# Packed softmax for six of eight units of a windowed attention that feeds an MLP

## The chip, the core and the metric

The kernel runs on one core of a Trainium2 chip. The metric is the device time of a run in microseconds; before the change three runs gave 794.72, 796.49 and 797.60 us. The profiler's own execution took 798.29 us, of which 796.3 lie between the first and the last instruction (the span). The engines are named as the profile names them: PE is TensorE (matmuls; PEld are its weight loads), DVE is VectorE, ACT is ScalarE, POOL is GpSimd, SP is SyncE, which only issues transfers here.

## The reference

Attention of 4 batches x 8 heads over 768 positions with head size 64; each query sees the first `n_sink` = 4 keys and the last `window` = 128 keys up to its own. What comes out goes, as 3072 tokens of width 512, through an MLP with a leaky ReLU.

```python
scores = scale * np.matmul(q, k.transpose(0, 1, 3, 2))
keep = is_sink | in_window                     # pos < n_sink, 0 <= rel < window
scores = np.where(keep, scores, -1000000000.0)
a = np.exp(scores - np.max(scores, axis=-1, keepdims=True))
a = a / (np.sum(a, axis=-1, keepdims=True) + 1e-09)
x = np.matmul(a, v)                            # then (B*S, H*D)
h = x @ w_in                                   # 512 -> 2048
out = np.maximum(0.01 * h, h) @ w_out          # 2048 -> 512
```

## The kernel before

**Units.** The work is cut into 8 units (`NU`): a batch has two, its first 384 queries (half 0) and its last 384 (half 1). A unit has 4 pairs of heads (`NPAIR`) and three query tiles of 128 (`T`). A query tile sees two key blocks of 128, the one before its own and its own, and the 4 sink keys: a score tile is 128 x 260 (`W3`), columns 0 to 127 the block before, 128 to 131 the sinks, then its own block. The first tile of half 0 sees only its own block (128 columns).

**Attention of a pair.** `scores` (L220 for the first two units, which are "native": fp32 products, two heads side by side; L225 for the others, where a head's q and k were split by `split_head` into a high part and a remainder) writes a tile into bank `s0` or `s1`. L235 on VectorE adds the mask, keeps the negative row maximum `negm` and writes `pk`; L239 on ScalarE takes the exponential and the row sum `sm`. L242 on GpSimd copies the 4 sink columns out to `sk`. `turn` transposes each 128 x 128 block of `pk` on TensorE (L260) into bank `t`, and L266 or L268 copies it to `pt` in SBUF. `gather` transposes `sk` (L274) into the same bank `t`, and L278 and L279 write it out as `st` in two parts; `gather` also inverts the sums (L283, L284) and spreads them (L286) to `rb`, which `spread` transposes (L293), again in bank `t`, and copies to `r`. `values` multiplies `pt` by the values (L306), adds the sink part (L310, one matmul), multiplies by `r` (L313) and splits the result into `xh` and `xl` (L316, L317), the inputs of the MLP.

**MLP of a unit.** For each of 16 blocks of 128 hidden columns: 12 matmuls of 384 columns into bank `h` (L399); L406 on ScalarE and L407 on VectorE form `g`; L408 on ScalarE and L409 form its two parts `gh` and `gl` (L409 is VectorE's for the first unit, GpSimd's later); one block later 9 matmuls of 512 columns (L421) add into the three output banks. The weights arrive as raw 64-bit words; during the opening and the first unit's MLP VectorE decodes each block in three steps (L125, L127, L129, all in the tile `w`), and ScalarE and GpSimd split it. In units 2 to 5 `check_weights` loads the raw words again, 32 blocks in all, and reduces them on ScalarE, GpSimd (L144) and VectorE (L146).

**What sets the order.** TensorE's order is written by hand: the program runs one step of `mlp_stream` after the other and between them, by the count `due`, steps of `attention_stream`, a few ahead of the unit that needs them. In `attention_stream` a step is a score tile, or one deferred function (`turn`, `gather`, `spread`, `values`) from the list `pend`, taken by a credit and a lag. The other engines' orders, SP's among them, come from the tile framework's scheduler; every engine works through its list in order. PSUM has 8 banks, each used by name: `h`, `s0`, `s1`, `t`, `v`, `o0`, `o1`, `o2`. SBUF tiles rotate by tag: `raw` (3 buffers, raw words and q/k), `io` (3, decoded words, output tiles, the check), `qksp`, `pk`, `pt`, `v`.

## Time and profile before

| | |
|---|---|
| median of 3 runs | 796.49 us (794.72 to 797.60) |
| profiled execution | 798.29 us, span 796.3 us |
| PE busy | 730.3 us, 92% |
| DVE, ACT, POOL busy | 403.9, 354.1, 377.5 us |
| mean clock granted to PE | 0.976 of full speed |
| DMA | 72.75 MB, mean 91 GB/s |

Busy time is the time in which at least one instruction of an engine runs. Matmuls overlap each other, so what one costs among others is the distance from its start to the next start. "Idle ... <- X" in a row means that the engine stood still and that X's end released it.

### The profile page before, as it was taken

The page shows a single profiled execution, that of the slowest core. Times are in us where ns is not written, and L with a number is a line of the kernel's source. Part 1 is how long each engine was busy: PE and PEld are TensorE (multiplying, and loading weights), DVE is VectorE, ACT ScalarE, POOL GpSimd, SP SyncE. Part 2 cuts the span into 40 slices and gives each one's busy share as a digit, 9 for nine tenths or more (in the row PEclk, how much of TensorE's full clock was granted, in tenths as well). Part 3 has the DMA queues.
Part 4 walks back from the last instruction along what each step waited for, and adds up shares of the span by engine and source line. Part 5 has one row for each costly group of instructions (what it writes and reads, how often), then busy time and mean ns, then how long its engine had stood idle before and what let it go on. Part 6 is the DMA issues. An engine that isn't in the chain of part 4 may idle for free. (4 is left out here: it accounts for less than half of the span.)

```text
span 796.3 us, 11589 instructions
## 1 busy us (share of the span) xinstructions
PE 730.3 (92%) x4109; PEld 614.6 (77%) x4109; DVE 403.9 (51%) x1070; ACT 354.1 (44%) x910; POOL 377.5 (47%) x473
## 2 busy tenths in 40 slices
PE   4798878999999899989999899998999999999996
PEld 3466666788888777878787788777788888888894
DVE  5979989753445444463444544445444544422111
ACT  3665545543444454454454454454454445322221
POOL 2525556434444655655655656545655544222221
PEclk9799999999999999999999999999999999999998
DMA  5626455221113423333322322224323220001001
GB/s 171 218 92 204 157 168 171 90 90 48 57 41 104 135 81 91 93 97 109 101 90 90 138 91 88 82 78 149 115 63 111 62 75 14 1 1 40 1 1 44
DMA packets 26034, 72.75 MB, mean 91 GB/s; under 512 B 3024, under 2 KB 5328, under 8 KB 25968
## 3 DMA queue, kind: packets, MB, share of 16 engines
q1 hardware_dynamic: 25824, 71.80, 27.8%
q8 instruction: 34, 0.56, 0.3%
q14 instruction: 32, 0.26, 0.1%
q10 hardware_dynamic: 144, 0.13, 0.0%
HBM read 65.63 MB, written 6.29 MB: 90 GB/s over the span
## 5 line engine op out<-in xcount | busy, mean ns | idle before, releaser
L399 PE MATMUL h<-xh,wih 128*128 128x384 f32 x512 | 185.0, 361 | 5.6 <-DVE g L407 5.4
L399 PE MATMUL h<-xl,wih 128*128 128x384 f32 x512 | 173.3, 338 | 0.0
L399 PE MATMUL h<-xh,wil 128*128 128x384 f32 x512 | 173.3, 338 | 0.0
L421 PE MATMUL o<-woh,gh 128*128 128x512 f32 x384 | 161.7, 421 | 0.0
L421 PE MATMUL o<-woh,gl 128*128 128x512 f32 x384 | 153.0, 398 | 1.8 <-DVE gl L409 1.5
L409 POOL TENSOR_TENSOR gl<-g,gh 128x384 fp32r<-128x384 f32 x112 | 113.4, 1013 | 84.8 <-ACT gh L408 83.8
L421 PE MATMUL o<-wol,gh 128*128 128x512 f32 x384 | 152.4, 397 | 0.0
L242 POOL COPY sk<-pk 128x36 f32<-128x36 f32 x160 | 45.4, 286 | 196.4 <-ACT pk L239 196.3
L407 DVE TENSOR_TENSOR g<-h,g 128x384 f32<-128x384 f32 x128 | 70.6, 552 | 122.9 <-ACT g L406 121.5
L235 DVE CUSTOM_DVE_ANT_0 pk<-s,m 128x260 f32<-128x260 f32 (+1 forms) x192 | 75.9, 402 | 112.2 <-PE s L225 102.8
L406 ACT ACTIVATE g<-h 128x384 f32<-128x384 f32 x128 | 62.3, 487 | 154.1 <-PE h L399 151.9
L239 ACT ACTIVATE pk<-pk,negm 128x260 f32<-128x260 f32 (+1 forms) x192 | 94.2, 491 | 58.9 <-DVE negm L235 58.7
L399 PEld LDWEIGHTS h<-xh,wih 128*128 128x128 f32 x512 | 97.7, 191 | 12.4 <-DVE g L407 7.5
L268 DVE COPY pt<-t 128x128 f32<-128x128 f32 (+1 forms) x168 | 67.0, 399 | 70.7 <-PE t L260 68.2
L399 PEld LDWEIGHTS h<-xl,wih 128*128 128x128 f32 x512 | 98.1, 192 | 3.3
L399 PEld LDWEIGHTS h<-xh,wil 128*128 128x128 f32 x512 | 97.3, 190 | 0.0
L421 PEld LDWEIGHTS o<-woh,gl 128*128 128x128 f32 x384 | 72.8, 190 | 20.2 <-DVE gl L409 2.4
L188 POOL TENSOR_TENSOR qksp<-qkraw,qksp 64x392 fp32r<-64x392 f32 (+1 forms) x48 | 57.3, 1194 | 64.1 <-issue 62.0
L408 ACT CAST gh<-g 128x384 fp32r<-128x384 f32 x128 | 65.4, 511 | 43.8 <-DVE g L407 40.7
L260 PE MATMUL t<-ident,pk 128*128 128x128 f32 x352 | 69.2, 284 | 11.6 <-DVE pt L268 11.5
L421 PEld LDWEIGHTS o<-woh,gh 128*128 128x128 f32 x384 | 72.9, 190 | 8.6 <-issue 0.7
L421 PEld LDWEIGHTS o<-wol,gh 128*128 128x128 f32 x384 | 73.2, 191 | 7.0
(88 smaller groups left out, 933.6 us busy)
## 6 DMA issues: line engine op xcount, KB each, us to landing
craw<-in_wq SPq DMA_DIRECT2D x32, 512.0 KB, 3.6
qkraw<-in_qk SPq DMA_DIRECT2D x24, 454.0 KB, 3.3
qkraw<-in_qk SPq DMA_DIRECT2D x24, 388.0 KB, 3.3
wiraw<-in_wq SPq DMA_DIRECT2D x16, 512.0 KB, 3.9
woraw<-in_wq SPq DMA_DIRECT2D x16, 512.0 KB, 3.6
out<-ob SPq DMA_DIRECT2D x23, 256.0 KB, 2.1
v<-in_vu SPq DMA_DIRECT2D x16, 256.0 KB, 2.7
v<-in_vu SPq DMA_DIRECT2D x16, 192.0 KB, 2.3
```

Source lines behind the costliest of these rows:

```text
L188: nc.gpsimd.tensor_tensor(out=sp[D:P, TU:TU + n], in0=raw[D:P, TU:TU + n], in1=sp[D:P, TU:TU + n].bitcast(F32), op=ALU.subtract)
L235: anchor[0] = nc.vector.tensor_tensor_reduce(out=w[:, 0:kn], in0=ps[:, 0:kn], in1=masks[min(T * (u % 2) + j, 2)], scale=-SCALE, scalar=3.0 ...
L239: nc.scalar.activation(out=w[:, 0:kn], in_=w[:, 0:kn], func=AF.Exp, scale=-1.0, bias=neg, accum_out=state["sm"][:, j, o:o + 1])
L242: nc.gpsimd.tensor_copy(out=state["sk"][:, j, :, o, :], in_=w[:, P:WM].rearrange("p (o s) -> p o s", o=1).broadcast_to([P, SKG, NSK]))
L260: nc.tensor.transpose(out=tp[:, i * m + c * P:i * m + (c + 1) * P], in_=w[:, a:z], identity=ident)
L268: nc.vector.tensor_copy(out=dst, in_=src)
L399: nc.tensor.matmul(ph[:, 0:TU], lhsT=w[:, cs], rhs=x, start=cc == 0 and c == 0, stop=cc == NCC - 1 and c == 2)
L406: nc.scalar.mul(g, ph[:, 0:TU], 0.01)
L407: anchor[0] = nc.vector.tensor_tensor(out=g, in0=ph[:, 0:TU], in1=g, op=ALU.max)
L408: nc.scalar.copy(out=gh, in_=g)
L409: (nc.gpsimd if u else nc.vector).tensor_tensor(out=gl, in0=g, in1=gh.bitcast(F32), op=ALU.subtract)
L421: nc.tensor.matmul(po[t], lhsT=gg[:, tsl], rhs=w, start=f == 0 and c == 0, stop=f == NFC - 1 and c == 2)
```

## The change

From the third unit on (`not native(u)`) the softmax of a tile is packed. A query at place q of its tile sees keys 0..q of its own block and keys q+1..127 of the block before, 128 in all, so both fit in one block: `copy_predicated` (L411) writes the scores of the block before over the own block's columns where key > query (mask `tri`), in PSUM, and `soft` works on 132 columns, the 4 sinks and the packed block. After a head's third tile the three row sums are inverted (L418, L419) and the three tiles multiplied by them in one instruction (L420): one normalisation a head. `turn_packed` transposes three blocks a head and writes them to `pt` twice, times `low` and times `upp` (L299): the part that belongs to the block before and the part that belongs to the own block. `rb`, its transpositions and `r` remain for the two native units only. The sinks of a pair go through one transposition (L304), and `load_sinks` fetches, for each pair, a 96 x 384 tile with one column group a query tile; the sink part of `acc` is 2 or 3 matmuls of 128 columns (L332).

The steps of attention are timed by counting score tiles: a deferred function is due `LAGT` or `LAGV` tiles later. Bank `v` goes; bank `d` holds the decoded word between the three decode steps, and from the third unit on `t` and `d` take turns for transpositions, sinks and `acc`. In the native units both heads' turned blocks leave in one ScalarE copy (L282). The first unit's `gl` and the native units' `xl` are GpSimd's.

```diff
-LAG = 3
-LAG0 = 2
-PKB = 6
-RATE = 3
-CAP = 2.5
+LAGT = 2
+LAGV = 3
...
+    tri = cpool.tile([P, P], I8, name="tri")
+    low = cpool.tile([P, P], F32, name="low")
+    upp = cpool.tile([P, P], F32, name="upp")
+    nc.vector.tensor_scalar(out=tri, in0=rel[:, P:], scalar1=0.0, scalar2=None, op0=ALU.is_lt)
+    nc.gpsimd.memset(low, 1.0)
+    nc.gpsimd.affine_select(out=upp, in_=low, pattern=[[1, P]], base=0, channel_multiplier=-1,
+                            compare_op=ALU.is_ge, fill=0.0)
+    nc.gpsimd.affine_select(out=low, in_=low, pattern=[[-1, P]], base=-1, channel_multiplier=1,
+                            compare_op=ALU.is_ge, fill=0.0)
+    pm = [m0]
+    for i, m in enumerate((m1, m2)):
+        pk = cpool.tile([P, W1], F32, name=f"pm{i}")
+        nc.gpsimd.tensor_copy(out=pk[:, 0:NSK], in_=m[:, snk])
+        nc.vector.tensor_tensor(out=pk[:, NSK:], in0=m[:, prv], in1=m[:, cur], op=ALU.max)
+        pm.append(pk)
+    return lim, (m0, m1, m2), pm, tri, low, upp
...
-            top, low = raw[:, :, 1], raw[:, :, 0]
+            top, low_ = raw[:, :, 1], raw[:, :, 0]
             w = iopool.tile([P, 512], F32, tag="io", name=f"w{nm}{fc}", bufs=3)
-            wi = w.bitcast(I32)
+            d = bank("d", f"d{nm}{fc}").bitcast(I32)
             with tc.issue_after(anchor[0].ins):
-                nc.vector.tensor_scalar(out=wi, in0=top, scalar1=3, scalar2=0x3FFFFFFF,
+                nc.vector.tensor_scalar(out=d, in0=top, scalar1=3, scalar2=0x3FFFFFFF,
                                         op0=ALU.logical_shift_left, op1=ALU.bitwise_and)
-            nc.vector.scalar_tensor_tensor(out=wi, in0=top, scalar=-0x40000000, in1=wi,
+            nc.vector.scalar_tensor_tensor(out=d, in0=top, scalar=-0x40000000, in1=d,
                                            op0=ALU.bitwise_and, op1=ALU.bitwise_or)
-            nc.vector.scalar_tensor_tensor(out=wi, in0=low, scalar=29, in1=wi,
+            nc.vector.scalar_tensor_tensor(out=w.bitcast(I32), in0=low_, scalar=29, in1=d,
                                            op0=ALU.logical_shift_right, op1=ALU.bitwise_or)
...
-    def load_sinks(b):
-        raw = iopool.tile([SKR, NPAIR * P], F32, tag="io", name=f"svr{b}", bufs=3)
-        nc.sync.dma_start(out=raw, in_=vs[b])
-        sv = apool.tile([SKR, NPAIR * P], F32R, tag="sv", name=f"sv{b}", bufs=1)
+    def load_sinks(u, pair):
+        raw = iopool.tile([SKR, TU], F32, tag="io", name=f"svr{u}_{pair}", bufs=3)
+        nc.sync.dma_start(out=raw, in_=vs[u // 2, pair])
+        sv = apool.tile([SKR, TU], F32R, tag="sv", name=f"sv{u}_{pair}")
         nc.scalar.copy(out=sv, in_=raw)
-        nc.vector.tensor_tensor(out=sv[D:SKR, :], in0=raw[D:SKR, :], in1=sv[D:SKR, :].bitcast(F32),
-                                op=ALU.subtract)
-        svs[b] = sv
+        (nc.gpsimd if native(u) else nc.vector).tensor_tensor(out=sv[D:SKR, :], in0=raw[D:SKR, :],
+                                                              in1=sv[D:SKR, :].bitcast(F32), op=ALU.subtract)
+        svs[u, pair] = sv
 
     def split_head(u, h):
         n = NK[u % 2]
...
     def turn_bank(u, name):
-        tags = ("t", "o2") if u == 0 else ("t",)
+        tags = (("t", "o2"), ("t",), ("t", "d"))[min(u, 2)]
         seq["t"] += 1
         return bank(tags[(seq["t"] - 1) % len(tags)], name)
...
+        anchor[0] = nc.vector.tensor_tensor_reduce(out=w, in0=src, in1=mask, scale=-SCALE, scalar=3.0e38,
+                                                   op0=ALU.add, op1=ALU.min, accum_out=neg)
+        nc.scalar.activation(out=w, in_=w, func=AF.Exp, scale=-1.0, bias=neg, accum_out=sm)
...
+    def turn_packed(u, pair, o, w, state):
+        half = u % 2
+        tp = turn_bank(u, f"t{u}_{pair}_{o}")
         for j in range(T):
...
+            nc.tensor.transpose(out=tp[:, j * P:(j + 1) * P], in_=w[:, j, NSK:], identity=ident)
+        pt = state["pt"][:, o]
+        src = tp[:, 0:TU].rearrange("p (j q) -> p j q", j=T)
+        if half:
+            dst = pt
+        else:
+            nc.scalar.copy(out=pt[:, 0:P], in_=tp[:, 0:P])
+            dst, src = pt[:, P:5 * P], src[:, 1:T]
+        dst = dst.rearrange("p (j t q) -> p t j q", t=2, q=P)
+        n = T - 1 + half
+        for t, mask in enumerate((low, upp)):
+            nc.vector.tensor_tensor(out=dst[:, t], in0=src,
+                                    in1=mask.rearrange("p (o q) -> p o q", o=1).broadcast_to([P, n, P]), op=ALU.mult)
+
+    def gather(u, pair, state):
+        tp = turn_bank(u, f"sk{u}_{pair}")
+        nc.tensor.transpose(out=tp[0:SKR, 0:P], in_=state["sk"].rearrange("p r j h s -> p (r j h s)"),
+                            identity=ident)
+        if native(u):
+            for j in range(T):
+                nc.tensor.transpose(out=tp[:, (j + 1) * P:(j + 2) * P],
+                                    in_=state["rb"][:, 2 * j:2 * j + 2].rearrange("p h d -> p (h d)"),
+                                    identity=ident)
+            r = xpool.tile([P, TU], F32, tag="r", name=f"r{u}_{pair}", bufs=1)
+            nc.scalar.copy(out=r, in_=tp[:, P:])
+            state["r"] = r
+        st = xpool.tile([SKR, P], F32R, tag="st", name=f"st{u}_{pair}")
+        nc.scalar.copy(out=st, in_=tp[0:SKR, 0:P])
+        nc.vector.tensor_tensor(out=st[32:D, :], in0=tp[32:D, 0:P], in1=st[32:D, :].bitcast(F32), op=ALU.subtract)
+        state["st"] = st
...
-        q0 = 0 if half else P
-        acc = bank("v", f"acc{u}_{pair}")
+        acc = turn_bank(u, f"acc{u}_{pair}")
         vv = vraws.pop((u, pair))
         for kb, (po, qo, m) in enumerate(segments(half)):
             for o in range(2):
                 nc.tensor.matmul(acc[o * D:(o + 1) * D, qo:qo + m],
                                  lhsT=vv[:, kb * P + o * D:kb * P + (o + 1) * D],
-                                 rhs=state["pt"][o][:, po:po + m], start=kb == 0, stop=False,
+                                 rhs=state["pt"][:, o, po:po + m], start=kb == 0, stop=False,
                                  skip_group_check=True)
-        nc.tensor.matmul(acc[:, q0:TU], lhsT=svs[u // 2][:, pair * P:(pair + 1) * P],
-                         rhs=state["st"][:, 0:TU - q0], start=False, stop=True, skip_group_check=True)
-        xf = state["r"]
-        nc.vector.tensor_tensor(out=xf, in0=acc[:, 0:TU], in1=xf, op=ALU.mult)
+        sv = svs.pop((u, pair))
+        for j in range(1 - half, T):
+            js = slice(j * P, (j + 1) * P)
+            nc.tensor.matmul(acc[:, js], lhsT=sv[:, js], rhs=state["st"], start=False, stop=j == T - 1,
+                             skip_group_check=True)
         xh = xpool.tile([P, TU], F32R, tag=f"xh{pair}", name=f"xh{u}_{pair}")
         xl = xpool.tile([P, TU], F32R, tag=f"xl{pair}", name=f"xl{u}_{pair}")
-        nc.scalar.copy(out=xh, in_=xf)
-        nc.vector.tensor_tensor(out=xl, in0=xf, in1=xh.bitcast(F32), op=ALU.subtract)
+        if native(u):
+            xf = state["r"]
+            nc.vector.tensor_tensor(out=xf, in0=acc[:, 0:TU], in1=xf, op=ALU.mult)
+            nc.scalar.copy(out=xh, in_=xf)
+            nc.gpsimd.tensor_tensor(out=xl, in0=xf, in1=xh.bitcast(F32), op=ALU.subtract)
+        else:
+            nc.scalar.copy(out=xh, in_=acc[:, 0:TU])
+            nc.vector.tensor_tensor(out=xl, in0=acc[:, 0:TU], in1=xh.bitcast(F32), op=ALU.subtract)
...
+                    load_sinks(u, pair)
+                count[0] += 1
+                if j == T - 1:
+                    spread(u, pair, state)
+                later(LAGT, lambda j=j, w=w: pt_then(turn_native, u, pair, j, w, state))
...
+                h = 2 * pair + o
+                sp = split_head(u, h)
+                fetch(o)
+                if o:
+                    load_sinks(u, pair)
+                w = apool.tile([P, 2 * W3], F32, tag="pk", name=f"pk{u}_{h}", bufs=3)
+                w = w[:, 0:T * W1].rearrange("p (j k) -> p j k", j=T)
+                sm = apool.tile([P, T], F32, tag="sm", name=f"sm{u}_{h}")
                 for j in range(T):
                     ps, = scores(u, pair, j, (o,), sp)
-                    ws = {o: softmax(u, pair, j, o, ps, state)}
+                    if KSL[u % 2][j][1] == W3:
+                        nc.vector.copy_predicated(out=ps[:, W1:W3], mask=tri, data=ps[:, 0:P])
+                        src = ps[:, P:W3]
+                    else:
+                        src = ps[:, 0:W1]
+                    soft(u, h, j, w[:, j], src, pmasks[min(T * (u % 2) + j, 2)], sm[:, j:j + 1])
+                    count[0] += 1
+                    if j == T - 1:
+                        nc.vector.tensor_scalar(out=sm, in0=sm, scalar1=1e-9, scalar2=None, op0=ALU.add)
+                        nc.vector.reciprocal(out=sm, in_=sm)
+                        nc.vector.tensor_tensor(out=w, in0=w, in1=sm.rearrange("p (j o) -> p j o", o=1)
+                                                .broadcast_to([P, T, W1]), op=ALU.mult)
+                        nc.gpsimd.tensor_copy(out=state["sk"][:, :, 0:T, o, :],
+                                              in_=w[:, :, 0:NSK].rearrange("p (r j) s -> p r j s", r=1)
+                                              .broadcast_to([P, 3, T, NSK]))
+                        later(LAGT, lambda o=o, w=w: pt_then(turn_packed, u, pair, o, w, state))
                     yield
-                    pend.append(lambda j=j, ws=ws: turn(u, pair, j, ws, state))
-        pend.append(lambda: gather(u, pair, state))
-        pend.append(lambda: spread(u, pair, state))
-        pend.append(lambda: values(u, pair, state))
+        later(LAGT, lambda: gather(u, pair, state))
+        later(LAGV, lambda: values(u, pair, state))
...
+                    while pend and pend[0][0] <= count[0]:
+                        pend.pop(0)[1]()
                         yield
...
-                (nc.gpsimd if u else nc.vector).tensor_tensor(out=gl, in0=g, in1=gh.bitcast(F32),
-                                                              op=ALU.subtract)
+                nc.gpsimd.tensor_tensor(out=gl, in0=g, in1=gh.bitcast(F32), op=ALU.subtract)
...
-    steps = [NPAIR * ((T if native(u) else 2 * T) + (T if native(u) else 2 * T) + 3) for u in range(NU)]
+    steps = [NPAIR * (2 * T + 2 if native(u) else 2 * T + 4) for u in range(NU)]
```

Two arrays change with it in the host's layout: the key columns of half 0 begin with the sinks, and `vs` holds, per batch and pair, 96 rows (3 copies of 4 x 2 x 4) by 3 x 128 columns.

**TensorE, a pair of the sixth unit (half 1).** Names: `sk` sinks, `r` inverted sums, `t` turned probabilities, `h` and `o` the MLP. Before, from the sinks' transpositions on:

```order
L274 MATMUL sk_1_4990<-ident,sk_1_4624 72x128 x3
L421 MATMUL o_0_4752<-woh_710,gh_4_4940 128x512
L421 MATMUL o_0_4752<-wol_711,gh_4_4940 128x512
L421 MATMUL o_0_4752<-woh_710,gl_4_4941 128x512
L421 MATMUL o_1_4753<-woh_710,gh_4_4940 128x512
L421 MATMUL o_1_4753<-wol_711,gh_4_4940 128x512
L421 MATMUL o_1_4753<-woh_710,gl_4_4941 128x512
L293 MATMUL r_1_5007<-ident,rb_1_4999 128x128 x3
```

Now, from the second head's turned blocks to the sinks' transposition:

```order
L288 MATMUL t_3_1_5218<-ident,pk_7_5085 128x128 x3
L485 MATMUL o_1_4642<-woh_1196,gh_10_5159 128x512
L485 MATMUL o_1_4642<-wol_1197,gh_10_5159 128x512
L485 MATMUL o_1_4642<-woh_1196,gl_10_5160 128x512
L485 MATMUL o_2_4643<-woh_1196,gh_10_5159 128x512
L485 MATMUL o_2_4643<-wol_1197,gh_10_5159 128x512
L485 MATMUL o_2_4643<-woh_1196,gl_10_5160 128x512
L464 MATMUL h_12_5237<-xh_0_3664,wih_1341 128x384
L464 MATMUL h_12_5237<-xl_0_3665,wih_1341 128x384
L464 MATMUL h_12_5237<-xh_0_3664,wil_1342 128x384
L304 MATMUL sk_3_5241<-ident,sk_133 96x128
```

Before, six matmuls of `o` stand between the two sets of transpositions that share bank `t`. Now nine MLP matmuls stand between the turned blocks (bank `d`) and the sinks (bank `t`), and no transposition follows the sinks.

**VectorE at the same places.** Names: `st` the sinks' second part, `zero` the weight check, `g` the MLP's activation, `sm` row sums. Before:

```order
L407 TENSOR_TENSOR g_5_4983<-h_5_4963,g_5_4983 128x384
L146 ISA zero_9_5019,wmin<-mag_9_5018,zero_9_5019 128x512
L146 ISA wmin 128x1
L279 TENSOR_TENSOR st_1_4994<-sk_1_4990,st_1_4994 32x384
L235 ISA pk_5_0_5038,negm<-s_5_0_5035,m_84 128x260
L235 ISA negm 128x1
L313 TENSOR_TENSOR r_1_5011<-acc_1_5048,r_1_5011 128x384
```

Now, the end of a head's softmax:

```order
L411 COPY_PREDICATED s_7_2_5145<-tri,s_7_2_5145 128x128
L251 ISA pk_7_5085,negm<-s_7_2_5145,pm_106 128x132
L251 ISA negm 128x1
L194 TENSOR_TENSOR sv_0_5312<-svr_0_5310,sv_0_5312 32x384
L472 TENSOR_TENSOR g_10_5158<-h_10_5128,g_10_5158 128x384
L418 TENSOR_SCALAR sm_7_5086<-sm_7_5086 128x3
L251 ISA pk_0_5179,negm<-s_0_0_5181,m_82 128x132
L251 ISA negm 128x1
L419 RECIPROCAL sm_7_5086<-sm_7_5086 128x3
L420 TENSOR_TENSOR pk_7_5085<-pk_7_5085,sm_7_5086 128x396
```

Before, the check stands right ahead of `st`. Now the sums and the multiply of a head (L418 to L420) stand among the next head's first reduces, behind a sink word's subtraction (L194) and a `g`.

**The first unit's MLP, fourth block.** VectorE before:

```order
L127 SCALAR_TENSOR_TENSOR wo_855<-woraw_853,wo_855 128x512
L407 TENSOR_TENSOR g_3_891<-h_3_863,g_3_891 128x384
L129 SCALAR_TENSOR_TENSOR wo_855<-woraw_853,wo_855 128x512
L317 TENSOR_TENSOR xl_0_879<-r_0_835,xh_0_878 128x384
L409 TENSOR_TENSOR gl_3_893<-g_3_891,gh_3_892 128x384
L235 ISA pk_4_0_906,negm<-s_4_0_902,m_84 128x260
```

GpSimd now:

```order
L149 TENSOR_TENSOR wil_882<-wi_876,wih_881 128x512
L340 TENSOR_TENSOR xl_0_870<-r_0_818,xh_0_869 128x384
L149 TENSOR_TENSOR wol_893<-wo_887,woh_892 128x512
L194 TENSOR_TENSOR sv_2_950<-svr_2_948,sv_2_950 32x384
L474 TENSOR_TENSOR gl_3_918<-g_3_916,gh_3_917 128x384
L387 COPY sk_131<-pk_2_0_937 128x3x4 x2
```

The subtraction that ends in `gl` has moved from VectorE, behind the decode (L125 to L129), to GpSimd, behind the weights' second parts (L149) and a sink word (L194).

## Rows read from the trace of the kernel before

**Rows 1.** The page's first part: busy us, share of the span, instructions.

```profile
PE 730.3 (92%) x4109; PEld 614.6 (77%) x4109; DVE 403.9 (51%) x1070; ACT 354.1 (44%) x910; POOL 377.5 (47%) x473
```

**Rows 2.** Stretches: length, busy us of PE, PEld, DVE, ACT, POOL; clock, DMA, GB/s.

```profile
0.00:52.15 52.15, 36.68 (x209) 22.41 (x209) 37.62 (x129) 27.74 (x92) 17.94 (x41) 0.84 0.51 173
52.15:162.60 110.45, 94.87 (x517) 75.52 (x515) 100.48 (x196) 57.15 (x138) 57.80 (x61) 0.97 0.46 151
250.05:347.10 97.05, 90.49 (x525) 78.00 (x524) 46.52 (x128) 45.96 (x118) 54.48 (x67) 0.98 0.31 98
347.10:442.00 94.90, 88.48 (x500) 75.54 (x499) 43.48 (x127) 44.24 (x116) 53.41 (x62) 0.98 0.32 100
442.00:539.20 97.20, 90.52 (x526) 78.04 (x525) 46.56 (x129) 45.98 (x118) 54.93 (x68) 0.98 0.30 98
539.20:631.50 92.30, 86.70 (x500) 74.16 (x498) 43.49 (x127) 44.33 (x116) 53.35 (x62) 1.00 0.32 102
```

**Rows 3.** PE's waits (us, times, longest): whole run, first MLP stage, opening.

```profile
PE r L293 <- DVE st L279: 25.8, 23, 2.4
...
PE t L260 <- DVE pt L268: 6.0, 4, 3.8
PE h L399 <- DVE g L407: 5.4, 3, 2.9
...
PE t L260 <- DVE pt L268: 3.9, 2, 2.5
```

**Rows 4.** Timeline around one wait: start us, us, engine, line, instruction.

```profile
308.65 1.41 DVE L146 CUSTOM_DVE_ANT_0 zero<-mag,zero 128x512 f32<-128x512 f32 x1
...
310.10 0.55 DVE L279 TENSOR_TENSOR st<-sk,st 32x384 fp32r<-32x384 f32 x1
...
310.70 0.55 PE L293 MATMUL r<-ident,rb 128*128 128x128 f32 x3 [1.54 <-DVE st L279]
```

**Rows 5.** Timeline of PE, 304.2 to 305.3 us.

```profile
304.26 0.39 PE L421 MATMUL o<-wol,gh 128*128 128x512 f32 x1
304.49 0.39 PE L421 MATMUL o<-woh,gl 128*128 128x512 f32 x1
304.72 0.38 PE L260 MATMUL t<-ident,pk 128*128 128x128 f32 x2
304.86 0.42 PE L399 MATMUL h<-xh,wih 128*128 128x384 f32 x1
305.12 0.34 PE L399 MATMUL h<-xl,wih 128*128 128x384 f32 x1
305.29 0.34 PE L399 MATMUL h<-xh,wil 128*128 128x384 f32 x1
```

**Rows 6.** Groups by shape: busy us, mean ns | idle before.

```profile
L235 DVE CUSTOM_DVE_ANT_0 pk<-s,m 128x260 f32<-128x260 f32 x160 | 67.2, 426 | 85.0 <-PE s L225 78.8 <-PE s L220 3.5 <-PE t L260 0.6
...
L409 DVE TENSOR_TENSOR gl<-g,gh 128x384 fp32r<-128x384 f32 x16 | 14.3, 897 | 2.6 <-ACT gh L408 2.6
...
L239 ACT ACTIVATE pk<-pk,negm 128x128 f32<-128x128 f32 x32 | 12.7, 399 | 21.1 <-DVE negm L235 21.1
...
L235 DVE CUSTOM_DVE_ANT_0 pk<-s,m 128x128 f32<-128x128 f32 x32 | 8.8, 285 | 27.2 <-PE s L225 23.9 <-PE s L220 3.2
```

**Rows 7.** Single lines: count, shortest/median/longest in ns.

```profile
L127 DVE SCALAR_TENSOR_TENSOR wo<-woraw,wo x16: 673/688/1769, 16.3 to 143.1; 128x512 int32<-128x512 int32 x16
...
L268 DVE COPY pt<-t x168: 250/424/426, 15.6 to 701.5; 128x256 f32<-128x256 f32 x140, 128x128 f32<-128x128 f32 x28
...
L283 DVE TENSOR_SCALAR sm<-sm x32: 157/443/1268, 14.3 to 696.0; 128x6 f32<-128x6 f32 x32
...
L317 DVE TENSOR_TENSOR xl<-r,xh x32: 544/549/1370, 30.0 to 708.9; 128x384 fp32r<-128x384 f32 x32
...
L407 DVE TENSOR_TENSOR g<-h,g x128: 511/557/560, 55.7 to 784.7; 128x384 f32<-128x384 f32 x128
...
L409 POOL TENSOR_TENSOR gl<-g,gh x112: 993/1013/1028, 167.1 to 785.9; 128x384 fp32r<-128x384 f32 x112
```

More of the change, by code (lines that the diff above doesn't have):

```diff
@@ L77, in build_masks @@
                    allow_small_or_imprecise_dtypes=True)
-    m0 = cpool.tile([P, P], F32, name="m0")
+    m0 = cpool.tile([P, W1], F32, name="m0")
     m1 = cpool.tile([P, W3], F32, name="m1")
     m2 = cpool.tile([P, W3], F32, name="m2")
-    prv, cur = m1[:, 0:P], m1[:, WM:]
-    nc.vector.tensor_scalar(out=cur, in0=rel[:, P:], scalar1=0.0, scalar2=None, op0=ALU.is_ge)
-    nc.vector.scalar_tensor_tensor(out=cur, in0=rel[:, P:], scalar=win, in1=cur, op0=ALU.is_lt, op1=ALU.mult)
-    nc.vector.scalar_tensor_tensor(out=m0, in0=key, scalar=ns, in1=cur, op0=ALU.is_lt, op1=ALU.max)
+    prv, snk, cur = slice(0, P), slice(P, W1), slice(W1, W3)
@@ L91, in build_masks @@
[L91 removed]
+    nc.gpsimd.tensor_copy(out=m2, in_=m1)
+    nc.vector.tensor_scalar(out=m2[:, snk], in0=key[:, 0:NSK], scalar1=ns, scalar2=-1.0, op0=ALU.is_lt,
                             op1=ALU.add)
[L93 to L94 removed]
+    nc.vector.tensor_scalar(out=m2[:, snk], in0=m2[:, snk], scalar1=MASKED, scalar2=None, op0=ALU.mult)
@@ L200, in keep_warm @@
             nc.tensor.matmul(warm[:, 0:2 * P], lhsT=wz[:, 0:P], rhs=wz, start=True, stop=True)
+    for i in range(2):
+        sks.append(wpool.tile([P, 3, 4, 2, NSK], F32, name=f"sk{i}"))
+        nc.gpsimd.memset(sks[i], 0.0)
     seq = {"s": 0, "t": 0}
@@ L249, in segments, with spread @@
         return (0, 0, 2 * P), (2 * P, P, 2 * P), (4 * P, 2 * P, P)
[L251 to L281 removed]
+    def spread(u, pair, state):
         sm = state["sm"]
@@ L288, in gather, with turn_native @@
         state["rb"] = rb
-    def spread(u, pair, state):
-        tp = turn_bank(u, f"r{u}_{pair}")
-        for j in range(T):
-            nc.tensor.transpose(out=tp[:, j * P:(j + 1) * P],
-                                in_=state["rb"][:, 2 * j:2 * j + 2].rearrange("p h d -> p (h d)"), identity=ident)
-        r = xpool.tile([P, TU], F32, tag="r", name=f"r{u}_{pair}", bufs=1)
-        nc.scalar.copy(out=r, in_=tp[:, 0:TU])
-        state["r"] = r
+    def turn_native(u, pair, j, w, state):
+        half = u % 2
+        kn = KSL[half][j][1]
+        tp = turn_bank(u, f"t{u}_{pair}_{j}")
+        cols = (0, W1) if kn == W3 else (NSK,)
+        m = P * len(cols)
+        o0 = 2 * P * j if half else max(2 * j - 1, 0) * P
+        for o in range(2):
+            for c, a in enumerate(cols):
+                nc.tensor.transpose(out=tp[:, o * m + c * P:o * m + (c + 1) * P], in_=w[:, o, a:a + P],
+                                    identity=ident)
+        if u == 0:
+            keep_warm(1)
+        nc.scalar.copy(out=state["pt"][:, :, o0:o0 + m], in_=tp[:, 0:2 * m].rearrange("p (o q) -> p o q", o=2))
@@ L321, in ahead, with later, fetch, tile_pt @@
         return (u, pair + 1) if pair < NPAIR - 1 else (u + 1, 0)
+    count = [0]
     def attend(u, pair, pend):
-        state = {"sm": apool.tile([P, T, 2], F32, tag="sm", name=f"sm{u}_{pair}"),
-                 "sk": apool.tile([P, T, SKG, 2, NSK], F32, tag="sk", name=f"sk{u}_{pair}"),
-                 "pt": [apool.tile([P, 2 * TU], F32, tag="pt", name=f"pt{u}_{2 * pair + o}", bufs=3)
-                        for o in range(2)]}
+        state = {"sk": sks[pair % 2]}
         nxt = ahead(u, pair)
-        if pair == 0 and u % 2 == 0:
-            load_sinks(u // 2)
+        def later(lag, f):
+            pend.append((count[0] + lag, f))
+        def fetch(o):
+            if nxt[0] < NU and o == 0:
+                load_values(*nxt)
+            if native(u) and nxt[0] < NU and native(nxt[0]):
+                load_pair(*nxt)
+            elif not native(u) and o == 0:
+                load_head(u, 2 * pair + 1)
+            elif nxt[0] < NU:
+                load_head(nxt[0], 2 * nxt[1])
+        def tile_pt():
+            if "pt" not in state:
+                state["pt"] = apool.tile([P, 2, 2 * TU], F32, tag="pt", name=f"pt{u}_{pair}", bufs=1)
+        def pt_then(f, *args):
+            tile_pt()
+            f(*args)
@@ L371, in attention_stream @@
                     yield
-                    credit = min(credit + RATE, CAP)
-                    while credit >= 1.0 and len(pend) > (LAG0 if native(u) else LAG):
-                        credit -= 1.0
-                        pend.pop(0)()
+                    while pend and pend[0][0] <= count[0]:
+                        pend.pop(0)[1]()
                         yield
-        for f in pend:
+        for _, f in pend:
             f()
@@ L635, in layout @@
     vu1 = vp[:, :, :, 2:6].reshape(B, NPAIR, P, 4 * P)
-    vs = np.zeros((B, SKR, NPAIR, 2, D), v.dtype)
+    vs = np.zeros((B, NPAIR, 3, 4, 2, NSK, T, 2, D), v.dtype)
     s4 = v[:, :, 0:NSK].reshape(B, NPAIR, 2, NSK, D)
-    for r in (0, 32, 64):
-        for x in range(2):
-            vs[:, r + x * NSK:r + (x + 1) * NSK, :, x] = s4[:, :, x].transpose(0, 2, 1, 3)
-    vs = vs.reshape(B, SKR, NPAIR * P)
+    for r in range(3):
+        for j in range(T):
+            for x in range(2):
+                vs[:, :, r, j, x, :, j, x] = s4[:, :, x]
+    vs = vs.reshape(B, NPAIR, SKR, TU)
     wi, wo = c(moe_w_in), c(moe_w_out)
```

105 lines of the change are left out of this document (31 added, 74 removed).

## The prediction, made before the changed kernel ran

> **What bounds the kernel now.** I read the first part of the page, then a table of busy time by stage, then who waits for whom on TensorE, and last the engines around one such wait in order of time. TensorE is busy 730.3 us of the span of 796.3 [rows 1]: its own work is the floor, and a change is worth what it takes out of that work and out of the 66 us in which TensorE stands still.
>
> The stages [rows 2] are the opening (attention of the first unit, no MLP yet) to 52.2 us; the first unit's MLP, 110.5 us; and the later MLPs with the attention of the next unit beside them. Two kinds of stage lose time. In the first MLP stage TensorE is busy 94.9 of 110.5 us and VectorE 100.5: VectorE decodes the weights there, and the others wait for it. In the four stages from 250.1 to 631.5 us TensorE idles 6.6, 6.4, 6.7 and 5.6 us, and its clock is at 0.98 of full in three of them. In the code these four are the units that check the weights.
>
> The waits name the place. In the whole run TensorE waited 25.8 us, 23 times, for `st` of L279 before the transpositions L293 [rows 3], nearly all of what the four stages idle. The timeline shows why [rows 4]: VectorE enters the weight check L146 at 308.65 for 1.41 us, `st` runs only at 310.10, and L293 starts at 310.70 after 1.54 us of idling, because `sk`, whose bank `st` must empty, and `r` share the one bank `t`. In the order of before six matmuls stand between the two.
>
> **The change part by part.** *Transpositions.* From the third unit on a head has 3 probability transpositions in place of 5 or 6, the sinks of a pair have one for 2 or 3, and L293 goes. The order of both kernels counts them: 352 to 232, 80 to 32, 96 to 24, so 240 fewer. The price comes from six starts [rows 5]. Matmuls of L421 start 0.23 us apart, those of L399 0.17. From 304.49 to 305.12 there are one of L421, two transpositions and one of L399: 0.63 - 0.23 - 0.17 = 0.23, so 0.115 each. 240 x 0.115 = 27.6 us, on the engine that sets the end. Against it stand 80 sink matmuls of 128 columns for 32 wider ones; the 48 more cost between nothing and 48 x 0.115 = 5.5; I take 1, since they carry hardly more columns.
>
> *The wait for `st`.* With L293 gone nothing on TensorE follows `sk` closely: `st` is next needed by the last matmuls of `acc`, behind 15 MLP matmuls, a score and the value products. So 25 of the 25.8 us go, and with the pauses the lower clock behind them: 2% of three stages is 5.8 at most, I take 4. Late next is the chain of a head: its third score, the predicated copy, the reduce, the exponential, two operations on the sums, the multiply over 396 columns, then the transpositions. With two scores of 260 columns at L421's pace per column, the rest from [rows 6, 7], by the nearest row where one is missing, that is 0.24 + 0.29 + 0.29 + 0.40 + 0.88 + 0.57 = 2.7 us without queueing. The order gives the second head of a pair 27 MLP matmuls and two scores before its transpositions: 15 x 0.17 + 12 x 0.23 + 2 x 0.24 = 5.8 us. Three us are left for queueing; a weight check takes 1.4 of them.
>
> *VectorE.* A pair of the longer half took 6 x 0.43 + 6 x 0.42 + 0.55 + 0.88 + 0.56 + 0.55 = 7.6 us. Now it has six reduces and six predicated copies at 0.29 (the copies have no row; a 128-column copy takes 0.25, a wider reduce 0.43, and I take the reduce of 128 columns), two pairs of sums at 0.88, two multiplies at 0.57, four masked copies at 0.56, and `st`, `xl` and the sink word, 1.4 together: 3.5 + 1.8 + 1.1 + 2.2 + 1.4 = 10.0. Four pairs add 10 us to the 46.5 of the stage at 250.1, which is 56 of some 84: off the path. ScalarE and GpSimd lose work there.
>
> [...] The subtraction L317, with both inputs in SBUF, takes 0.54 us at least and 1.37 at most, the decode step L127 0.67 to 1.77, while L407, which reads one input from PSUM, never passes 0.56 [rows 7]. [...] At the worst value of L317 in every multiply VectorE would have 48 x (1.37 - 0.57) = 38 us more, or 6 a stage; the sum, with VectorE at 56 of 84, would not change by that, but the chain's slack of three us would shrink by 0.8, which the worst chain below takes in.
>
> *The first MLP stage.* 16 subtractions `gl`, 14.3 us of VectorE [rows 6], go to GpSimd, four `xl` at 0.55 too, and 12 copies of turned probabilities at 0.42 go to ScalarE: 14.3 + 2.2 + 5.0 = 21.5 of 100.5. The decodes may gain by their word in PSUM or lose (the first of the three steps may run faster between SBUF places); between L127's 0.67 and 1.77 I count nothing and leave 10 us either way to the bounds. VectorE then needs 79 of some 97 us and no longer bounds. TensorE waited there 6.0 us for VectorE's copies and 5.4 for `g` [rows 3]; of its 15.6 us of idling I take 11.5 off, and 2.5 for the clock, 0.97 before: 14 us (2 to 17).
>
> *Opening.* Of the waits for VectorE's copies the largest kind is 3.9 us [rows 3]; these copies are ScalarE's now, twice as wide, and ScalarE was busy 27.7 of 52. I take a gain of 2 us (a loss of 4 to a gain of 6).
>
> *New waits.* A sink load for each pair, in the buffers of the decoded weights and on SyncE's queue, with a cast and a subtraction that stand in the order of ScalarE and of VectorE or GpSimd, and behind them whatever these engines owe TensorE; bank `d`; one `pt` tile. None is in the trace: 0 to 40 us (at the upper end 1.25 a pair, a little over the 25.8 / 23 = 1.1 us of a wait for `st`); I take 8, a quarter of a us a pair.
>
> Sum against the profiled execution, 798.3 (span 796.3): -27.6 + 1 - 25 - 4 - 14 - 2 + 8 = -63.6, so 734.7. It lay 1.8 above the median of the runs shown, so 733 us.
>
> **The rivals.** *The wait moves.* VectorE has 10 us more in each checked stage, and a late head chain or a late sink load stops TensorE as `st` did. For it: engines that work in order, and checks of 1.4 us. Against: three us of slack where six matmuls gave 1.4. Then the 29 us stay, and half of the first stage's gain: -27.6 + 1 - 7 - 2 = -35.6, less 1.8: 761.
>
> *GpSimd bounds the first MLP stage.* It was busy 57.8 us there and gets 16 `gl` at 1.01 [rows 7], four `xl` and four sink words at about the same: 82 of 97, in order, with a sink word that waits for its load ahead of a `gl`. The stage then gains nothing: 733 + 14 = 747.
>
> *The worst head chain.* With the sums at 1.27, the multiply at 1.37, a sink word at 1.37, a check at 1.41 and a `g` at 0.56 ahead, it takes 2.7 + 0.8 + 0.8 + 1.4 + 1.4 + 0.6 = 7.7 us, 1.9 beyond the order's 5.8, for the 24 second heads: 46 us, 779.
>
> *Slower: the predicated copy.* No row shows one; 120 of them stand between score and reduce. Without them VectorE has 8.3 us for a long pair and 4 of MLP and check ((46.5 - 4 x 7.6) / 4), against TensorE's (90.5 - 44 x 0.115 - 2) / 4 = 20.9: it bounds from 1.4 us a copy, the length of a check. At 2.4 us it needs 26.7 for a long pair and 21.3 for a short one (against 20.7): 12 x 5.8 + 12 x 0.6 = 77 us on top, 810. Against it: VectorE rows of 128 columns lie near 0.3 us.
>
> That the change does not do what it says is excluded for the transpositions: the order counts them.
>
> **How the numbers follow.** Forecast 0.59; the wait moves 0.17; GpSimd bounds 0.12; the worst chain 0.05; the slow copy 0.07. The forecast's own range: with every favourable bound 27.6 + 25.8 + 5.8 + 17 + 6 = 82 us go, 714; with 20 us of new waits it is 745. To hold 8 in 10 it takes in the rivals at 747 and 761 with some excess: 714 to 770. What a measurement can tell from no change is 0.3%, 2.4 us. Slower 0.06 and the same 0.03 come from the slow copy and the far end of the worst chain; faster is the rest, 0.91.
>
> **What would show it.** Right: 192 matmuls fewer; the stages from 250 to 632 us at 81 to 84 us each with idling under 2 us and clock 1.00; no wait for `st` over 1 us; the first MLP stage near 96 us with VectorE under 85% busy. Wrong: TensorE waiting for VectorE's multiply or masked copies ahead of transpositions or `acc`; GpSimd near full from 50 to 150 us; a predicated copy above 1 us; ScalarE, VectorE or GpSimd waiting for a sink load.

## The result and the profile after

The changed kernel took 726.0 us (median of 4 runs, 724.0 to 726.4) against 795.6 (794.7 to 797.6) for the kernel before: 0.9117 of its time, 95% interval 0.9091 to 0.9143. The prediction was 733, within 714 to 770. The profiled execution took 725.98 us, its span 724.1 against 796.3. The profiled execution before lay 2.7 us above its median, so differences between stages, which come from the profiles, add up to 72.2 us and not to 69.6.

The first part of the page after, beside [rows 1]; columns as there:

```profile
PE 691.5 (95%) x3917; PEld 591.5 (82%) x3917; DVE 430.3 (59%) x1189; ACT 349.2 (48%) x938; POOL 378.9 (52%) x425
```

TensorE has the announced 192 matmuls fewer, is busy 38.8 us less, and idles 32.6 us where it idled 66. The stretches of [rows 2] after the change (opening, first MLP stage, then three later stages; length, busy time of the engines, clock):

```profile
0.00:47.65 47.65, 32.68 (x209) 20.49 (x209) 30.69 (x116) 31.48 (x97) 26.19 (x66) 0.93 0.61 204
47.65:142.00 94.35, 90.57 (x519) 73.84 (x518) 79.77 (x174) 58.16 (x143) 69.90 (x82) 1.00 0.54 181
142.00:224.21 82.21, 82.21 (x472) 72.52 (x470) 48.25 (x140) 39.33 (x107) 37.38 (x41) 1.00 0.23 74
224.21:309.28 85.07, 83.83 (x489) 73.62 (x488) 54.55 (x156) 42.98 (x118) 50.44 (x49) 1.00 0.35 116
309.28:395.32 86.04, 83.83 (x469) 71.80 (x468) 54.85 (x155) 43.59 (x122) 49.90 (x49) 1.00 0.36 118
```

So the opening gave 4.5 us, the first MLP stage 16.1, and the four stages that check weights fell from 381.4 together to 340.7 (85.1, 86.0, 85.2 and 84.4, a little above the 81 to 84 that were announced). TensorE idles 1.1 to 2.2 us in each of the four, at clock 1.00. Its waits, beside [rows 3], whole run:

```profile
PE warm L215 <- POOL wz L210: 7.2, 1, 7.2
PE o L485 <- POOL gl L474: 5.7, 8, 1.3
PE h L464 <- DVE g L472: 3.2, 6, 1.7
PE acc L332 <- DVE sm L262: 3.2, 1, 3.2
...
PE acc L332 <- DVE st L316: 0.8, 2, 0.4
```

Of the 25.8 us for `st` 0.8 are left. The wait for `wz`, at the start, was 7.2 us before too; the largest new one is for `gl`. Groups by shape, beside [rows 6] (busy us, mean ns | idle before):

```profile
L474 POOL TENSOR_TENSOR gl<-g,gh 128x384 fp32r<-128x384 f32 x128 | 147.6, 1153 | 199.6 <-ACT gh L473 199.5
...
L420 DVE TENSOR_TENSOR pk<-pk,sm 128x396 f32<-128x396 f32 x48 | 52.0, 1084 | 1.3
L411 DVE COPY_PREDICATED s<-tri,s 128x128 f32<-128x128 int8 x120 | 35.7, 298 | 28.8 <-PE s L244 28.0
```

The predicated copy costs what a row of 128 columns suggested, the multiply nearly twice the 0.57 us taken. A sink load shows as an event of its own: ScalarE waited 35.1 us, 23 times, for sink loads (us, times, longest).

```profile
ACT sv L193 <- DMA svr<-in_vs: 35.1, 23, 6.0
```

### The profile page after: what moved, and what is told of

It is laid out like the page before. It is cut to its first block, busy times and chain, and to the rows that moved or that the text cites. A ratio compares the mean times of both kernels' runs of the same rounds, so it can differ in the third digit from the quotient of the medians.

```text
span 724.1 us, 11427 instructions
## 1 busy us (share of the span) xinstructions
PE 691.5 (95%) x3917; PEld 591.5 (82%) x3917; DVE 430.3 (59%) x1189; ACT 349.2 (48%) x938; POOL 378.9 (52%) x425
## 5 line engine op out<-in xcount | busy, mean ns | idle before, releaser
L474 POOL TENSOR_TENSOR gl<-g,gh 128x384 fp32r<-128x384 f32 x128 | 147.6, 1153 | 199.6 <-ACT gh L473 199.5
L464 PE MATMUL h<-xh,wih 128*128 128x384 f32 x512 | 180.3, 352 | 3.5 <-DVE g L472 3.2
L485 PE MATMUL o<-woh,gh 128*128 128x512 f32 x384 | 154.8, 403 | 0.0
L253 ACT ACTIVATE pk<-pk,negm 128x132 f32<-128x132 f32 (+1 forms) x192 | 81.4, 424 | 84.2 <-DVE negm L251 83.2
L464 PEld LDWEIGHTS h<-xl,wih 128*128 128x128 f32 x512 | 96.5, 188 | 4.9 <-POOL xl L340 0.5
L203 POOL TENSOR_TENSOR qksp<-qkraw,qksp 64x396 fp32r<-64x396 f32 (+1 forms) x48 | 56.5, 1177 | 72.2 <-issue 61.2
L159 POOL TENSOR_SCALAR zero<-mag 128x512 f32<-128x512 f32 x32 | 48.3, 1508 | 22.6 <-DMA out<-ob 14.8
L202 ACT CAST qksp<-qkraw 128x780 fp32r<-128x780 f32 (+1 forms) x48 | 43.1, 898 | 31.7 <-PE s L244 28.6
L244 PE MATMUL s<-qksp 128*128 128x260 f32 (+1 forms) x288 | 56.3, 277 | 0.0
L244 PEld LDWEIGHTS s<-qksp 128*128 128x128 f32 x288 | 52.8, 188 | 3.9
```

What stands on the lines that cost most here:

```text
L159: nc.gpsimd.tensor_scalar(out=zero, in0=mag, scalar1=0.0, scalar2=None, op0=ALU.is_equal)
L202: nc.scalar.copy(out=sp[:, 0:TU + n], in_=raw[:, 0:TU + n])
L203: nc.gpsimd.tensor_tensor(out=sp[D:P, TU:TU + n], in0=raw[D:P, TU:TU + n], in1=sp[D:P, TU:TU + n].bitcast(F32), op=ALU.subtract)
L244: nc.tensor.matmul(pss[0][:, 0:kn], lhsT=sp[:, off + j * P:off + (j + 1) * P], rhs=sp[:, TU + k0:TU + k0 + kn], start=c == 0, stop=c == 1)
L253: nc.scalar.activation(out=w, in_=w, func=AF.Exp, scale=-1.0, bias=neg, accum_out=sm)
L464: nc.tensor.matmul(ph[:, 0:TU], lhsT=w[:, cs], rhs=x, start=cc == 0 and c == 0, stop=cc == NCC - 1 and c == 2)
```

## The experiments

Times are medians. Beside each run stood the kernel before, at 795.2 to 795.4 us: a variant of the kernel before is compared with that, a variant of the changed kernel with 726.0. Ratios are to the kernel before.

**The wait for `st`: another order in the kernel before.**

```
+        norm(u, pair, state)           # the reciprocals and rb, cut out of gather
+        pend.append(lambda: spread(u, pair, state))
         pend.append(lambda: gather(u, pair, state))
-        pend.append(lambda: spread(u, pair, state))
```

> The kernel before with the same work in another order: the reciprocals right after the last softmax, and the transpositions of r ahead of those of sk, so that bank t is emptied for sk by ScalarE alone and st is not needed before the last matmul of acc. My account (the wait for st was the shared bank and the weight check ahead of st on VectorE): the 25.8 us go, with up to 5.8 of clock, less what a late copy of r costs: 795.6 - 26 to 31, so 765 to 770, and the four stages at 88 to 91 us. Rival (VectorE is late there whatever waits for it): acc waits for st in place of r, and the time stays above 785.

763.6 us, ratio 0.9604 (0.9574 to 0.9635): 31.8 us gone with the same instructions. One checked stage, and TensorE's waits in all four:

```profile
246.81:335.54 88.73, 88.41 (x527) 76.71 (x525) 46.49 (x128) 45.75 (x118) 54.37 (x67) 1.00 0.34 107
```

```profile
PE h L402 <- DVE g L410: 0.8, 2, 0.6
PE t L260 <- DVE pt L268: 0.6, 2, 0.4
PE sk L274 <- ACT r L298: 0.2, 1, 0.2
```

The four stages take 352.1 us in place of 381.4: 29.4 us for wait and clock, where the prediction had 25 + 4. TensorE idles 23.0 us less there and is busy 6.4 us less, at clock 1.00 where three of the four had 0.98 [rows 2]. The rival falls for these stages, where no wait is left above 0.6 us. Elsewhere `acc` now waits for `st`, as it said, but 3.8 us in all:

```profile
PE acc L312 <- DVE st L279: 3.8, 6, 1.7
```

**What held `st` up: the kernel before without its weight checks.** (The two lines that call `check_weights` are left out, and constants stand for its results.)

> The kernel before without its check of the weights (the loads, magnitudes, zeros and minima of the four checked units are left out; constants stand in their place). My account (the check ahead of st made the wait): the four stages fall from 381 us together to 4 x 87.5 = 350, as the stages without a check, so 795.6 - 31 = 764, with no wait for st over 1 us. Rival (the bank conflict costs the same without the check): 785 to 795.

769.2 us, ratio 0.9669 (0.9653 to 0.9685), 26.2 us gone; the four stages 354.5 together. The wait keeps its count and loses its size (whole run):

```profile
PE r L293 <- DVE st L279: 6.3, 23, 0.4
```

The bank sets up the wait 23 times, the check made it long: 2.4 us at most before, 0.4 now. Leaving the check out also takes work from ScalarE, GpSimd and the transfers, so that it is VectorE's part of it rests on [rows 4] and on the other order. Either cure takes most of the loss.

**The price of a transposition: 240 given back to the changed kernel.**

```
-        for j in range(T):
+        for j in (0, 1, 2, 0, 1, 2, 1, 2):
             nc.tensor.transpose(out=tp[:, j * P:(j + 1) * P], in_=w[:, j, NSK:], identity=ident)
```

> The changed kernel with five of the transpositions of every packed head done a second time into the same place: 240 more, nothing else. My account (a transposition costs 0.115 us of TensorE's path): 240 x 0.115 = 27.6 on 726.0, so 753.6, and TensorE busy about 719 of the span. Rival (the fewer transpositions gave little, the gain came from the waits): a transposition is partly hidden beside the weight loads or in pauses, at most 10 us in all, so 736 or less.

750.1 us, ratio 0.9424 (0.9400 to 0.9448): 24.1 us, 0.100 each. TensorE's busy time rose by 26.0, 0.108 each:

```profile
PE 717.5 (96%) x4157; PEld 618.1 (83%) x4157; DVE 430.7 (58%) x1189; ACT 351.4 (47%) x938; POOL 376.9 (50%) x425
```

Part of the difference is idling that fell from 32.6 to 31.2 us; the wait for `gl` went from 5.7 to 3.1. The six starts of [rows 5] had given 0.115.

**The second bank for the transpositions.** From the third unit on the banks of `turn_bank`, ("t", "d"), are ("t",) again.

> The changed kernel with its turned probabilities, sinks and acc from the third unit on all in the one bank t, as before the change. My account (the one shared bank made the wait): the sinks' transposition now follows the second head's turn in one bank and waits for its masked copies, and acc waits for st; at 1.1 us for each of 24 pairs 26 us, 752, and the named waits return. Rival (the distances in the order alone do it, since turn, sinks and values now stand a score tile or several MLP steps apart): 726 to 730, no wait over 1 us.

729.8 us, ratio 0.9169 (0.9149 to 0.9189): 3.8 us, and my account fell. The waits that came are small:

```profile
PE sk L304 <- ACT pt L282: 2.1, 2, 1.4
PE sk L304 <- DVE pt L299: 1.8, 4, 0.6
```

With the turned blocks, sinks and values apart in the order, the second bank is worth little: the order did it.

**How much slack a head's chain has.** `later(LAGT, ...)` of the packed turn becomes `later(1, ...)`.

> The changed kernel with the transpositions of a packed head one score tile after its last score in place of two. My account (the order gave the chain of a head 5.8 us, unloaded it needs 2.7, with its multiply at 1.1 in place of 0.57 some 3.3): half of the order's distance is about 2.9 us, so TensorE waits for the multiply at most of the 48 heads, 0.4 to 1.5 us each: 20 to 70 us, I say 755, and the wait named is t for pk of the multiply. Rival (the chain has so much slack that the distance doesn't matter): 726 to 730.

744.0 us, ratio 0.9344 (0.9305 to 0.9383): 18.0 us, less than I said, by the wait I named, at 13 heads:

```profile
PE t L288 <- DVE pk L420: 13.0, 13, 2.8
```

At two tiles this wait is 0.8 us, once. The prediction's slack exists, and half of the order's distance would not do. The other 5 us were not traced.

**The predicated copy, doubled.**

```
+                        for _ in range(2):
+                            nc.vector.copy_predicated(out=ps[:, W1:W3], mask=tri, data=ps[:, 0:P])
```

> The changed kernel with every predicated copy done twice in a row: 120 more, 0.30 us each. My account (VectorE is off the path from the third unit on, 55 of 85 us, and a head's chain has slack): 6 us more in a stage, 61 of 85: no change beyond 2 us, 726 to 728. Rival (the head's chain or VectorE decides): 20 copies of 0.3 us a stage, six stages, up to 36 us: 740 to 762.

730.0 us, ratio 0.9164 (0.9139 to 0.9190): 4.0 us, twice what I had allowed, for 35 us of VectorE. Off the path, but not free: TensorE's wait for `g`, which VectorE makes in the same queue as the copies, rose from 3.2 to 6.7 us.

**The first MLP stage: `gl` back on VectorE.**

```
-                nc.gpsimd.tensor_tensor(out=gl, ...)
+                (nc.gpsimd if u else nc.vector).tensor_tensor(out=gl, ...)
```

> The changed kernel with the subtraction gl of the first unit back on VectorE, as before the change; the decodes in the bank, the copies of turned probabilities on ScalarE and xl on GpSimd stay. My account (VectorE bounded the first MLP stage, and gl was the largest part of what it lost): VectorE needs 79.8 + 14.3 = 94 us of that stage again, and most of the 16 us come back: stage 104 to 108 us, whole 736 to 740. Rival (GpSimd bounds the stage now, with 69.9 us busy, in order and with spread): without 16 gl it gets shorter or stays, 94 us or less, 724 to 727. Second rival (the decodes in the bank and the copies gave the gain): stage 95 to 98, 727 to 730.

725.5 us, ratio 0.9113 (0.9089 to 0.9137): no change, and my account fell. The stage:

```profile
47.20:141.92 94.72, 91.40 (x519) 75.29 (x518) 86.47 (x190) 58.16 (x143) 56.60 (x66) 0.98 0.55 180
```

VectorE has 6.7 us more, GpSimd 13.3 less, and the length stays: TensorE, busy 91.4 of 94.7 us, bounds the stage either way. `xl` and the copies were not put back by themselves.

**The decode word back in SBUF.** `d = bank("d", ...)` becomes `d = w.bitcast(I32)`.

> The changed kernel with the intermediate word of the weight decode back in SBUF, in place of the PSUM bank d (which the turns keep). My account, which counted nothing for this edit: the three steps take 0.55 + 0.93 + 0.84 us in the mean in place of 2.07, 0.24 us on some 26 decodes, 6 us of VectorE, and VectorE is 86 of 94 us busy: stage 94 to 98, whole 726 to 730. Rival (the decode beside GpSimd bounded the stage): the steps spread to 1.8 us again and the stage gives back 8 to 16 us, 734 to 742.

745.4 us, ratio 0.9370 (0.9342 to 0.9397): 19.4 us lost, more than the rival's 8 to 16, and my account fell. The stage is longer than before the change [rows 2], though `gl`, `xl` and the copies have left VectorE:

```profile
50.00:162.74 112.74, 97.23 (x519) 79.05 (x518) 91.78 (x174) 58.23 (x143) 82.08 (x82) 0.94 0.46 151
```

The timeline of VectorE and GpSimd there (start us, us, engine, line, instruction) shows both long side by side:

```profile
63.48 1.57 POOL L149 TENSOR_TENSOR wol<-wo,woh 128x512 fp32r<-128x512 f32 x1 [0.38 <-ACT woh L148]
...
63.82 1.77 DVE L142 SCALAR_TENSOR_TENSOR wi<-wiraw,wi 128x512 int32<-128x512 int32 x1
...
65.01 1.45 POOL L474 TENSOR_TENSOR gl<-g,gh 128x384 fp32r<-128x384 f32 x1
...
65.52 1.50 DVE L142 SCALAR_TENSOR_TENSOR wo<-woraw,wo 128x512 int32<-128x512 int32 x1
...
66.94 0.68 DVE L144 SCALAR_TENSOR_TENSOR wi<-wiraw,wi 128x512 int32<-128x512 int32 x1
```

L142 takes 0.68 us at least, L149 1.26, and `gl` took 0.99 at the least in the changed kernel. Here the first L142 ends 0.54 us after L149 does, the second 0.56 us after `gl`; L144, with GpSimd idle, takes its 0.68. With the word in PSUM no L142 takes more than 0.70 us, though of the 64 runs of L142 and L144 there 62 overlap a GpSimd instruction (shortest/median/longest in ns; first line with the word in SBUF, the others the changed kernel):

```profile
L142 DVE SCALAR_TENSOR_TENSOR wi<-wiraw,wi x16: 680/1237/1775, 14.9 to 141.4; 128x512 int32<-128x512 int32 x16
...
L142 DVE SCALAR_TENSOR_TENSOR di<-wiraw,di x16: 686/696/697, 15.4 to 120.3; 128x512 int32<-128x512 int32 x16
L142 DVE SCALAR_TENSOR_TENSOR do<-woraw,do x16: 685/691/697, 18.2 to 122.5; 128x512 int32<-128x512 int32 x16
```

The kernel before shows the same: of its 64 runs of L127 and L129, 25 overlap no GpSimd instruction, and these take 0.68 to 0.69 us; every longer one, up to 1.79, overlaps one. The three decode steps hold VectorE for 68.0 us of this stage, against 53.9 in the changed kernel. A second reading would be that the early steps wait for a buffer that GpSimd still reads; but VectorE waited for one here only once, for 1.2 us, and never in the kernel before.

**The decode word in PSUM, alone, in the kernel before.** The word goes to bank `v`; `acc` of the first two units goes to the turn banks.

> The kernel before with one thing of the change alone: the intermediate word of the decode in a PSUM bank (bank v, while acc of the first two units goes through the turn banks). gl, xl and the copies stay on VectorE. The account I now hold (the word in PSUM gave the gain of the first MLP stage, because the decode and GpSimd no longer hold each other up): the decode falls from some 61 us to 54, without spread, GpSimd's subtractions too; the stage goes from 110.5 to 96 to 100 us, the whole from 795.4 to 780 to 785. Rival (the word in PSUM only pays once VectorE is relieved of gl, xl and the copies, 21.5 us): VectorE still needs 93 us and the stage stays at 104 or more, the whole above 788.

783.2 us, ratio 0.9851 (0.9821 to 0.9882): 12.0 us gone. The stage with `gl`, `xl` and all copies still on VectorE:

```profile
50.44:147.37 96.93, 90.20 (x517) 73.28 (x516) 91.60 (x196) 56.34 (x138) 49.91 (x60) 1.00 0.54 172
```

This one edit takes 13.5 us off the stage, the whole change 16.1. The decode steps fall from 59.7 us of VectorE to 53.5; the rest is the clock, 1.00 in place of 0.97, and shorter waits behind them: TensorE is busy 90.2 us there in place of 94.9 and idles 6.7 in place of 15.6, though VectorE is busy 91.6 of 96.9 us. That `acc` changes banks was not tried by itself; the run before this one, without that, points the same way.

**The multiply in three.** Three `tensor_scalar` of 132 columns by `sm[:, i:i + 1]` in place of L420.

> The changed kernel with the multiply of a head (396 columns, two inputs in SBUF, 1.08 us in the mean) written as three multiplies of 132 columns by a value per partition, so that each reads one tensor in SBUF. Account (the multiply's spread is two SBUF inputs against GpSimd): the three together take 0.6 to 0.8 us with no spread, GpSimd's longest gl falls below 1.1; the time changes by less than 3 us, 723 to 726. Rival (the spread has another cause): a multiply of 132 columns still spreads to twice its least. Rival for the time (GpSimd held up by the multiply makes the waits for gl): 720 to 722.

725.2 us, ratio 0.9126 (0.9102 to 0.9150): no change in time, as expected, but the account of the spread fell in this form (shortest/median/longest in ns):

```profile
L421 DVE TENSOR_SCALAR pk<-pk,sm x144: 274/704/1096, 126.0 to 621.9; 128x132 f32<-128x132 f32 x144
```

The spread, 0.27 to 1.10 us, is there with one tensor read in SBUF too: 51 of these overlap no GpSimd instruction and take 0.27 to 0.29 us, all longer ones overlap one. The three cost 88.0 us of VectorE in place of 52.0.

**Sink loads in a buffer of their own.**

```
-        raw = iopool.tile([SKR, TU], F32, tag="io", name=f"svr{u}_{pair}", bufs=3)
+        raw = iopool.tile([SKR, TU], F32, tag="svr", name=f"svr{u}_{pair}", bufs=1)
```

> The changed kernel with the sink loads in a buffer of their own, in place of the three that decoded weights, checks and outputs share. Account (ScalarE waits for sink loads 35.1 us, and what it owes behind that makes TensorE wait for gl 5.7 and for acc 3.2): these waits of ScalarE fall under 10 us, those of TensorE for gl under 2 and for acc in the opening under 1; 718 to 722. [...]

718.9 us (718.0 to 721.1), ratio to before 0.9046 (0.9020 to 0.9072): 7.1 us less than the changed kernel, and the fastest of all. TensorE's wait for `gl` in the four checked stages, in the changed kernel and then here; ScalarE's wait for sink loads here, whole run; and one of the stages:

```profile
PE o L485 <- POOL gl L474: 4.4, 6, 1.3
...
PE o L485 <- POOL gl L474: 1.3, 3, 0.6
...
ACT sv L193 <- DMA svr<-in_vs: 5.8, 1, 5.8
```

```profile
224.29:307.76 83.47, 83.47 (x490) 73.87 (x488) 53.36 (x156) 43.57 (x118) 50.32 (x49) 1.00 0.37 119
```

ScalarE waits once for a sink load, 5.8 us in place of 35.1. The gain is in the checked stages (334.3 us in place of 340.7, 82.6 to 84.1 each). The edit also leaves the three shared buffers to the checks and outputs alone; the run doesn't tell the two apart. In the opening nothing is gained: there the wait for `acc` goes, and one of 3.0 us for `r` of L338 takes its place.

**Both of these.**

> The changed kernel with both: sink loads in a buffer of their own and the multiply as three of 132 columns. If each account holds and the gains add: 717 to 721, and TensorE idles under 26 us of the span in place of 32.6. If the waits only move: 723 to 727.

720.1 us, ratio 0.9057 (0.9034 to 0.9079): not told apart from the own buffer alone. The gain is the buffer's.

## Why the prediction was right, and where it was not

The sign was right and the total 7 us short. The mechanism was right for the checked stages and the transpositions, and wrong for the first MLP stage. By its terms:

- *Transpositions, -27.6, sinks +1.* Giving 240 back cost 24.1 us. The size was 15% high: six starts are a small base. No run changes the sink matmuls alone; from each one's start to the next start on TensorE, the 32 of before take 8.6 us together and the 80 now 10.8, so about 2.2 in place of 1.
- *The wait for `st`, -25, and clock, -4.* The order alone gave 31.8 in the whole and 29.4 in the four stages, 23.0 of idling and 6.4 of busy time at the higher clock. The reading of [rows 4], the shared bank with a check ahead of `st`, held in both of its halves. That the wait would move (761) did not happen.
- *First MLP stage, -14.* The size came out near (-16.1) for the wrong reason, which is luck, and this is the step that failed: the gain was put on the 21.5 us that leave VectorE, and the decodes were counted at nothing. `gl` put back changes nothing; all 21.5 us moved, with the word in SBUF, leave a stage of 112.7 us, no shorter than the 110.5 before; the decode word in PSUM alone takes off 13.5. VectorE's share of the stage, 100.5 of 110.5 [rows 2], looked like work, but L127 and L129 in it took up to 1.79 us beside a GpSimd instruction, and 0.68 to 0.69 with none beside them. With the word back in SBUF the timeline has steps of 1.77 and 1.50 us in place of 0.68. The prediction said that the decodes may gain or lose by their word in PSUM and gave that no price, because the 0.67 to 1.77 us of L127 [rows 7] were taken as a bound either way. That the median there (0.69) lies by the shortest (0.67) hinted that the long ones had something beside them. Their sum would still have priced too little: the decodes' own 6.1 us are less than half of the 13.5.
- *GpSimd bounds that stage (747).* No: 69.9 us of 94.4, and TensorE 90.6. With the word back in SBUF it was busy 82.1 us, but of a stage of 112.7.
- *Opening, -2.* It gave 4.5, inside the bounds; its parts were not told apart.
- *New waits, +8.* Place right, and size near: ScalarE waits for sink loads, VectorE for ScalarE's copy of them (10.8 us, 12 times), a `gl` behind them comes late, and TensorE waits; a buffer of their own takes 7.1 us off. A ScalarE waiting for a sink load stood among the signs of being wrong; it came, within the 8 us allowed. Bank `d` and the one `pt` tile were not priced singly.
- *Chain of a head.* The multiply takes 1.08 us, not 0.57, and the slack still held; at half the distance it cost 18.0 us. The worst chain (779) was kept off by that distance.
- *Predicated copy.* 0.298 us, as the neighbouring rows had it; 810 fell with it. VectorE's forecast, 56 us in the stage at 250 us before, stands against 54.6.

Order, decode word and transpositions less sinks (24.1 - 2.2) are 31.8 + 12.0 + 21.9 = 65.7 us, from single edits to either kernel, of 69.6. They need not add: taking the word out of the changed kernel costs 19.4 us, putting it alone into the kernel before gained 12.0. With the word in SBUF, GpSimd is busy 82.1 us of the stage in the first case, where it has `gl` and `xl`, and 57.8 [rows 2] in the second. How the remaining 4 us divide was not settled.

## What to carry to other kernels

Before work is moved off a busy engine, look at the shortest, median and longest time of its instructions, and at what the long ones overlap. Where the longest is far above the shortest (here 1.77 us against 0.67, the long ones all beside GpSimd), an operand's place can be worth more than moving the work: here a word moved to PSUM took 13.5 us off a stage, and `gl` put back on VectorE changed nothing. A TensorE wait on a shared bank (25.8 us) was cured here by the order of the issues alone, a gain of 31.8 us; try that first. A new small load that shares buffers with rare long users (checks, outputs) gained 7.1 us here by a buffer of its own.
